# Row tiles transposed by DMA, paired last columns and an early inverse stage in a convolution and feed-forward kernel

## The chip, the cores and the metric

The kernel runs on one core of a Trainium2 chip. The metric is device time in microseconds, the median of the runs. A matrix engine (TensorE, PE in the profile), a vector engine (VectorE, DVE), an activation engine (ScalarE, ACT) and a general engine (GpSimd, POOL) work side by side, each through its own list of instructions in order; transfers are issued by one more list (SyncE, SP) and run on 16 DMA engines.

## What is computed

One layer of a sequence model over 2048 rows of 640 columns in bf16. A long convolution along the rows, done by Fourier transform, is gated by the normalised input, and a feed-forward layer of width 1728 follows:

```python
# kv = (4-tap shift of k) * v ; y = irfft(rfft(kv, 4096) * rfft(ssm_k, 4096))[:2048] + kv * ssm_D
h  = x + layernorm(x) * y
a  = einsum(layernorm(h), w1) + b1
h2 = h + einsum(a * tanh(softplus(a)), w2)
```

## The kernel before

**Tiles.** The transform is done in matmuls. A sequence of 2048 rows is split as 128 x 16; the first stage transforms over 128, the second over 16. Columns go in five chunks of 128, in three groups (two, two and one chunk). Row tile t2 is the 128 rows with the same remainder mod 16; there are 16 of them.

**The transform part.** The names are those of the operations in the code: `k1` transposes the convolution kernel on TensorE, `s1k` and `s2k` are its two transform stages, `kspe` the four shifts of k as small matmuls, `kv` the product with v on VectorE, `s1v` and `s2v` the stages of that, `prod` the product of both spectra, `i1` the inverse first stage. Each stage of matmuls writes into PSUM and is evicted as 1024 columns by ScalarE or VectorE (one helper, lines L390 and L392: the suffix `ev`). `prod` needs the kernel's spectrum twice, once with real and imaginary rows exchanged: 20 DMAs within SBUF (`d_swap`, L639) make the second copy, with real rows in partitions 0 to 63 and imaginary in 64 to 127. It runs as two instructions (L720), one for each copy. In the first stage (L510, L511) one 64-column weight is used twice, for the upper and the lower half of the output partitions. k is transposed as it is loaded, by DMA (`d_kT`, L476).

**The row chain.** For each row tile: the inverse second stage `i2pe` (L782, six matmuls into PSUM), the normalised x `lnx` on ScalarE (L789), their product `wb` on VectorE out of PSUM (L793), the sum `h` (L797), its statistics `ln2` (L802 and two more), the reciprocal root on GpSimd (L422), the normalised h `dr` (L812, into `hc`, a ring of three slots), five transposes on TensorE `trpe` (L819) and their eviction `trev` into `lnhT`.

**The feed-forward part.** Rows are taken in units of 128, 128, 256, 512, 512 and 512. For a unit, `m1pe` makes 14 chunks of 128 columns, five matmuls each (L845), ScalarE applies the activation (`hb`, L851), and `m2pe` multiplies each of the unit's row tiles by w2, 28 matmuls of 320 columns (L861); `res` adds h (L870) and a DMA stores the tile. 1728 is 13.5 x 128, so the last chunk is half zeros.

**The order.** A planner in the kernel (`_schedule`) takes operations by a table of priorities (`PRIO`) and estimated durations, picks the engine of each eviction and the PSUM bank, and emits the result; each engine's instructions then run in that order. 24 filler matmuls on zeros (`fill`, L830) may be put where TensorE is expected to be idle before the feed-forward part. All input loads, swaps and stores are on SP.

Of the kernel before, what the change touches and what calls it, by code (L numbers as in the profile page):

```python
# [17 lines left out]
D = 640  # L18
# [13 lines left out]
Q_R = "sp"  # L32
Q_V = "sp"
Q_SWAP = "sp"
KTP = 16 + S
PRIO = {
# [34 lines left out]
}  # L71
# [22 lines left out]
OFF_OB = OFF_XA + 3840  # L94

# [5 lines left out]

_CELL = {}
# [9 lines left out]
class _Op:  # L112
    __slots__ = ("name", "opts", "deps", "allocs", "emit", "prio", "lat", "start", "finish", "eng", "done", "picks", "cap", "xbar")

    def __init__(self, name, opts, deps, allocs, uses, emit, prio, lat):
        self.name = name
        self.opts = opts if isinstance(opts, list) else [opts]
        self.deps = deps
        self.allocs = list(allocs)
        for rt in list(allocs) + list(uses):  # L120
            rt.users.append(self)
        self.emit = emit
        self.prio = prio
        self.lat = lat
        self.start = None
        self.finish = None
        self.eng = None
        self.done = False
        self.cap = 0.0
        self.xbar = False  # L130

_WIN = 0.3
_SEM = 0.18
_OWN = {"act": 0.1, "dve": 0.1}
_FIRST = 0.6
_LAST_BYTE = 1.6

def _stage(name):
    m = re.match(r"(k1|s1k|s2k|kp|ks|kv|s1v|s2v|x|prod|i1|gb|d_swap|c_diag|d_kn|d_kT|d_R|d_v)(?:pe|ev)?(\d*)(?:_.*)?$", name)
    if not m:  # L140
        return name
    st = {"kp": "s2k", "x": "s2v"}.get(m.group(1), m.group(1))
    return st + m.group(2)

def _schedule(ops):
    _CELL.clear()
    free = {}
    order = []
    cap_free = 0.0
    ring_free = {}  # L150
    ring_sent = {}
    ndeps = {id(o): len(o.deps) for o in ops}
    children = {}
    for o in ops:
        for d in o.deps:
            children.setdefault(id(d), []).append(o)
    bl = {}
    for o in reversed(ops):
        m = 0.0
        for c in children.get(id(o), []):  # L160
            v = bl[id(c)] + o.lat
            if v > m:
                m = v
        bl[id(o)] = m + min(d for (_, d) in o.opts)
    ready = [o for o in ops if ndeps[id(o)] == 0]
    n_total = len(ops)
    while len(order) < n_total:
        cands = []
        for o in ready:
            t_dep = 0.0  # L170
            picks = []
            taken = set()
            for rt in o.allocs:
                best_slot = None
                for sl in rt.ring.slots:
                    if any(c in taken for c in sl):
                        continue
                    t = 0.0
                    for c in sl:
                        prev = _CELL.get(c)  # L180
                        if prev is None:
                            continue
# [744 lines left out]
```

## Time and profile before

| | us |
|---|---|
| median of 3 runs (242.58 to 244.99) | 244.71 |
| span of the profiled execution, first to last instruction | 238.7 |
| median less span | 6.0 |
| TensorE busy | 221.0 |
| VectorE busy | 155.5 |
| ScalarE busy | 139.5 |

The profile shows one execution. Busy times of TensorE include the latency of pipelined matmuls, so what one matmul costs is read from the starts of two neighbours or from the chain of waits, not from its own length. The chain follows what ended last back to its releaser, piece by piece. A group line gives count, busy time and mean length of one instruction in ns, then the idle time before it and who ended that.

### The profile page before, as it was taken

Reading aid. Unit: us, or ns where it says so; the run is one execution under the profiler, and the core shown is the slowest. Engines: PE = TensorE matmul, PEld = TensorE weight load, DVE = VectorE, ACT = ScalarE, POOL = GpSimd, SP = SyncE. Lnnn points to the kernel's source line nnn. Section 1 sums busy time; section 2 is a strip of 40 time slices with the busy share of each in tenths; the row PEclk is TensorE's granted clock in tenths of the full one; section 3 lists DMA queues with packets and bytes.
Section 4 is the critical chain, followed back from the end, with each engine's and each line's share of the span. In section 5 each row is a group of like instructions: output and inputs, shape, how many; then the busy total and the mean of one; then the engine's idle time right before and its main releaser. Section 6 shows DMA issues by size and latency. Waiting matters only on the chain.

```text
span 238.7 us, 7414 instructions
## 1 busy us (share of the span) xinstructions
PE 221.0 (93%) x3266; PEld 167.2 (70%) x3266; DVE 155.5 (65%) x318; ACT 139.5 (58%) x192; POOL 20.3 (9%) x39
## 2 busy tenths in 40 slices
PE   8888688988779999999999999999999999999993
PEld 3777577888779998698788764577744677545772
DVE  0998967899979998899999898584350332100121
ACT  2668676989998999589166456930156401366000
POOL 2500000000000003022311200210000000000000
PEclk9999999999999999999999999999999999999999
DMA  6999999806999797000000000001000001000001
GB/s 235 393 340 228 173 181 225 124 3 150 238 233 388 236 368 292 5 3 3 27 30 1 27 30 0 0 4 55 27 30 0 0 30 52 31 0 3 27 27 55
DMA packets 20049, 25.52 MB, mean 107 GB/s; under 512 B 11633, under 2 KB 15538, under 8 KB 19634
## 3 DMA queue, kind: packets, MB, share of 16 engines
q1 hardware_dynamic: 19760, 24.88, 37.5%
q8 instruction: 25, 0.41, 0.7%
q10 hardware_dynamic: 146, 0.18, 0.5%
q0 software_dynamic: 112, 0.01, 0.1%
q14 instruction: 6, 0.05, 0.1%
HBM read 14.57 MB, written 2.62 MB: 72 GB/s over the span
## 4 chain that ended last, share of the span: by engine, by line
PE 77%; ACT 10%; issue 4%; DVE 4%; DMA 3%; SPq 0%; ACTq 0%; DVEq 0%
PE banks L861 26%; PE banks L845 25%; ACT arena L390 9%; PE banks L539 6%; PE banks L731 4%; PE banks L732 4%; PE banks L782 3%; DMA arena<-tab_R 3%; PE banks L510 3%; PE banks L586 2%; DVE arena L392 2%; PE banks L819 2%; PE banks L560 1%; PE banks L830 1%; PE banks L511 1%
## 5 line engine op out<-in xcount | busy, mean ns | idle before, releaser
L390 ACT CAST arena<-banks 128x1024 bf16<-128x1024 f32 x78 | 73.2, 1046 | 16.3 <-PE banks L511 10.6
L845 PE MATMUL banks<-arena 128*128 128x512 bf16 (+2 forms) x420 | 62.3, 308 | 0.3 <-ACT arena L390 0.2
L861 PE MATMUL banks<-arena 128*128 128x320 bf16 x448 | 62.0, 299 | 0.2 <-DVE arena L793 0.2
L851 ACT ACTIVATE arena<-banks,b1s 128x512 bf16<-128x512 f32 (+2 forms) x84 | 43.5, 546 | 27.6 <-PE banks L845 25.5
L861 PEld LDWEIGHTS <-arena 128*128 128x128 bf16 x448 | 43.6, 98 | 17.1 <-issue 0.4
L845 PEld LDWEIGHTS <-arena 128*128 128x128 bf16 x420 | 35.3, 98 | 25.7 <-issue 0.7
L870 DVE TENSOR_TENSOR arena<-banks,arena 128x640 bf16<-128x640 f32 x16 | 13.2, 824 | 43.3 <-PE banks L861 43.2
L539 PE MATMUL banks<-arena 128*128 128x64 bf16 (+1 forms) x768 | 25.3, 188 | 4.6 <-ACT arena L390 2.9
L392 DVE CAST arena<-banks 128x1024 bf16<-128x1024 f32 x22 | 26.3, 1221 | 4.5 <-PE banks L511 2.2
L390 ACT COPY arena<-banks 128x640 bf16<-128x640 bf16 (+1 forms) x12 | 8.6, 746 | 32.7 <-PE banks L819 32.5
L539 PEld LDWEIGHTS <-arena 128*128 128x128 bf16 x768 | 23.3, 97 | 6.2 <-issue 5.1
L720 DVE TENSOR_TENSOR arena<-arena 128x1024 bf16<-128x1024 bf16 x40 | 24.8, 687 | 2.2 <-ACT arena L390 1.7
L510 PE MATMUL banks<-consts,arena 128*64 128x128 bf16 x320 | 21.3, 220 | 3.4 <-ACT arena L390 2.0
L511 PE MATMUL banks<-consts,arena 128*64 128x128 bf16 x320 | 21.6, 221 | 0.0
L511 PEld LDWEIGHTS <-arena 128*64 128x64 bf16 x320 | 18.4, 110 | 3.4 <-issue 3.2
L731 PE MATMUL banks<-consts,arena 128*128 128x128 bf16 x160 | 18.8, 219 | 1.3 <-DVE arena L392 0.9
L510 PEld LDWEIGHTS <-arena 128*64 128x64 bf16 x320 | 18.7, 110 | 1.7 <-issue 1.0
L732 PE MATMUL banks<-consts,arena 128*128 128x128 bf16 x160 | 18.7, 219 | 0.0
L732 PEld LDWEIGHTS <-arena 128*128 128x128 bf16 x160 | 15.6, 98 | 1.3 <-issue 1.0
L731 PEld LDWEIGHTS <-arena 128*128 128x128 bf16 x160 | 15.6, 98 | 0.6 <-issue 0.6
L789 ACT ACTIVATE arena<-arena,nmr_75,r1v 128x640 bf16<-128x640 bf16 x16 | 14.4, 926 | 2.6 <-DVE nmr_75 L684 1.4
L392 DVE COPY arena<-banks 128x1024 bf16<-128x1024 bf16 (+1 forms) x14 | 8.0, 598 | 11.8 <-PE banks L819 11.7
(47 smaller groups left out, 181.0 us busy)
## 6 DMA issues: line engine op xcount, KB each, us to landing
arena<-arena SPq DMA_DIRECT2D x20, 256.0 KB, 6.0
arena<-in_A_ssm_k_dram SPq DMA_DIRECT2D x5, 512.0 KB, 8.2
arena<-in_A_v_dram SPq DMA_DIRECT2D x2, 1280.0 KB, 15.4
arena<-in_A_q_dram SPq DMA_DIRECT2D x8, 320.0 KB, 5.6
out_dram<-arena SPq DMA_DIRECT2D x16, 160.0 KB, 1.8
arena<-in_B_w_dram SPq DMA_DIRECT2D x5, 432.0 KB, 8.4
arena<-in_B_w_dram SPq DMA_DIRECT2D x6, 320.0 KB, 4.8
arena<-tab_R SPq DMA_DIRECT2D x1, 1024.0 KB, 7.4
```

What stands on the lines that cost most here:

```text
L390: clock.append(nc.scalar.copy(o, i))
L392: nc.vector.tensor_copy(o, i)
L510: nc.tensor.matmul(ps1[0:64, gl, :], lhs, fcfs_b[:, 0, :], start=True, stop=True)
L511: nc.tensor.matmul(ps1[64:128, gl, :], lhs, fcfs_b[:, 1, :], start=True, stop=True)
L539: nc.tensor.matmul(ps2[:, c0:c0 + nd], G_t()[:, f0 + fl, :], src[:, f0 + fl, :], start=True, stop=True)
L720: nc.vector.tensor_tensor(kp, x, kp, ALU.mult)
L731: nc.tensor.matmul(pz[:, gl, :], KP_t()[:, dg, :], a12_b[:, 0, :], start=True, stop=False)
L732: nc.tensor.matmul(pz[:, gl, :], KPS_t()[:, dg, :], a12_b[:, 1, :], start=False, stop=True)
L789: nc.scalar.activation(lnx.tile, xn_t()[:, t2, :], ACT.Identity, scale=r1v[:, t2:t2 + 1], bias=nmr1[:, t2:t2 + 1])
L845: nc.tensor.matmul(ph[:, 0:w], w1_t()[:, dc, fc * P:(fc + 1) * P], lnhT_t()[:, dc, c0:c0 + w], start=(dc == 0), stop=(dc == NDC - 1))
L851: nc.scalar.activation(ub_t[u % 2]()[:, fc, 0:w], rt.tile[:, 0:w], ACT.Mish, bias=b1s[:, fc:fc + 1], scale=1.0)
L861: nc.tensor.matmul(po[:, hf2 * 512:hf2 * 512 + 320], hb[:, fc, tl * P:(tl + 1) * P], w2_t()[:, fc, hf2 * 320:(hf2 + 1) * 320], start=(fc = ...
```

## The change

Seven things change together.

- **Transposes by DMA.** For row tiles 2 to 15, `trpe` and `trev` are replaced by one DMA transpose each from `hc` into `lnhT` (`d_tr`, on SP). Tiles 0 and 1 stay on TensorE.
- **Last columns paired.** In units of more than 128 rows the last chunk is computed as 64 columns for the first half of the rows in output partitions 0 to 63 and for the second half in 64 to 127; the activation covers half the columns, and the second product takes the last 64 rows of w2 from a small tile `w2p` that holds them in either half, the rest zero. The bias of the last columns is loaded into both halves.
- **Inverse second stage ahead.** `i2pe` is split into `i2a` (groups 0 and 1, four matmuls of 256 columns for each row tile) and `i2b` (group 2, several row tiles in one bank). Their results are evicted as bf16 into SBUF (`ya`, `yb`), and `wb` reads them there. All but tile 10 stand before the first product.
- **Alternate rows.** Real and imaginary rows of the spectra alternate in the partitions; the swaps copy even to odd partitions and odd to even. The masked tables (`gb`) are written in contiguous pieces of 32.
- **`prod`** is one instruction over both copies, with the other spectrum broadcast.
- **Second product** in pieces of 512 and 128 columns; for the last row tile the two pieces are separate operations with an add and a store each.
- **Order.** Planner, priorities and fillers are gone. A written list (`ORDER`) gives each operation's engine, slot and place, and for some loads an instruction that they wait for (`pace`). Two small tiles move into the big one.

```diff
+        if t2 >= 2:
+            def trd(e, t2=t2, hc=hc):
+                return nc.sync.dma_start_transpose(lnhT_t()[:, :, t2 * P:(t2 + 1) * P], hc.tile)
+            o_td = DMA(f"d_tr{t2}", 164e3, trd, w=[("lnhT", t2)], prio=pr, after=[o_dr] + i1_pes, rate=160e3, xbar=True)
+            hc.users.append(o_td)
+            continue
...
-                    nc.tensor.matmul(ph[:, 0:w], w1_t()[:, dc, fc * P:(fc + 1) * P], lnhT_t()[:, dc, c0:c0 + w],
-                                     start=(dc == 0), stop=(dc == NDC - 1))
+                    if tail:
+                        for hh in range(2):
+                            nc.tensor.matmul(ph[64 * hh:64 * hh + 64, 0:w // 2], w1_t()[:, dc, fc * P:FF], lnhT_t()[:, dc, c0 + hh * (w // 2):c0 + (hh + 1) * (w // 2)],
+                                             start=(dc == 0), stop=(dc == NDC - 1))
+                    else:
...
-                for hf2 in range(2):
+                for a, b in parts:
                     for fc in range(NFC):
-                        nc.tensor.matmul(po[:, hf2 * 512:hf2 * 512 + 320], hb[:, fc, tl * P:(tl + 1) * P],
-                                         w2_t()[:, fc, hf2 * 320:(hf2 + 1) * 320], start=(fc == 0), stop=(fc == NFC - 1))
+                        wt = w2_t()[:, fc, a:b] if fc < NFC - 1 else w2p[:, 0, a:b]
+                        lo = tl * P
+                        if split and fc == NFC - 1 and lo >= w // 2:
+                            lo -= w // 2
+                            wt = w2p[:, 1, a:b]
+                        nc.tensor.matmul(po[:, a:b], hb[:, fc, lo:lo + P], wt, start=(fc == 0), stop=(fc == NFC - 1))
...
+        o = OP(f"i2ape{t2}", ("pe", 0.44), r=[("t2m", t2)] + [k for k in last_w if k[0] == "zb" and k[1] < 2], allocs=[rt], emit=pe, prio=41 + 0.01 * t2)
+        def yf(e, t2=t2, rt=rt):
+            return ev(e, yb(t2, 0, 512), rt.tile)
...
-            nc.vector.tensor_tensor(lnx.tile, rt.tile[:, 0:D], lnx.tile, ALU.mult)
+            return nc.vector.tensor_tensor(lnx.tile, yb(t2, 0, 640), lnx.tile, ALU.mult)
...
-                    a, b = (0, 64) if half == 0 else (64, 0)
-                    ENG_Q[Q_SWAP].dma_start(KPS_t()[a:a + 64, g0:g0 + 16, :].rearrange("p g f -> p (g f)"),
-                                      KP_t()[b:b + 64, g0:g0 + 16, :].rearrange("p g f -> p (g f)"))
+                    ENG_Q[Q_SWAP].dma_start(KPS_t()[half:P:2, g0:g0 + 16, :].rearrange("p g f -> p (g f)"),
+                                      KP_t()[1 - half:P:2, g0:g0 + 16, :].rearrange("p g f -> p (g f)"))
...
-                x = xa.tile[:, 0:nf * nd].rearrange("p (g f) -> p g f", f=nf)
-                for kt in (KP_t(), KPS_t()):
-                    kp = kt[:, d0:d1, f0:f0 + nf]
-                    nc.vector.tensor_tensor(kp, x, kp, ALU.mult)
+                x = xa.tile[:, 0:nf * nd].rearrange("p (g f) -> p g f", f=nf).unsqueeze(1).to_broadcast([P, 2, nd, nf])
+                kp = KK2_t()[:, :, d0:d1, f0:f0 + nf]
+                return (nc.gpsimd if e == "pool" else nc.vector).tensor_tensor(kp, x, kp, ALU.mult)
```

The written order around the passage into the feed-forward part and up to the fourth unit (name, engine, slots, what it waits for; some names left out):

```text
d_v1/sp// d_kT1/sp// ... d_v0/sp// d_kT0/sp// ... d_kT2/sp// ... d_kT3/sp// ... d_kT4/sp// ... d_swap0_0_48/sp//
...
i1ev1_0/act// i2bpe4/pe/0/ d_w2_12/sp//i1ev1_0 i1ev1_1/act// i2bpe0/pe/1/ ln1s2/pool// yb4/dve// i2bpe3/pe/2/ yb0/act// i2ape1/pe/3/ ln1f2/dve// yb3/dve// lnx2/act/2/ i2ape4/pe/0/ ya1/dve//
...
dr1/dve/0/ i2ape14/pe/0/ h0/dve// ya2/act// trpe1/pe/2/ ya14/act// i2ape11/pe/3/ trev1/dve// i2ape3/pe/1/ wb2/dve// ya11/act// m1pe1_6/pe/0/ ln2_0/dve//
...
dr3/dve/2/ hb0_8/act// m1pe0_4/pe/3/ ln2s_2/pool// hb0_6/act// ln1_4/dve// m1pe0_5/pe/2/ d_tr3/sp// hb0_4/act// m1pe0_3/pe/1/ hb0_5/act// m1pe1_13/pe/3/ hb0_12/act// i2ape10/pe/2/ hb0_3/act// hb1_13/act// dr2/dve/0/ m2pe0/pe/0/ ln1s4/pool// ya10/act// ln1_7/dve// d_tr2/sp//
...
dr4/dve/1/ ln2s_7/pool// ln2_6/dve// hb2_7/act// d_tr4/sp// m1pe2_10/pe/1/ hb2_4/act// m2pe1/pe/1/ dr7/dve/2/ hb2_10/act// ln2s_6/pool// ln2_5/dve// d_tr7/sp// dr6/dve/0/ ln2s_5/pool// d_tr6/sp// dr5/dve/1/ ln1_9/dve// d_tr5/sp// m2pe3/pe/0/
```

More of the change, by code (lines that the diff above doesn't have):

```diff
@@ L94 @@
 OFF_OB = OFF_XA + 3840
+NYA = 6
+OFF_YA = OFF_KK
+OFF_YB = OFF_G + 17920
 class _Ring:
@@ L247, in _schedule, with _replay @@
+        self.pace = ""
+        self.ins = None
+def _replay(ops):
+    by = {o.name: o for o in ops}
+    order = []
+    for tok in ORDER.split():
+        name, eng, slots, pace = tok.split("/")
+        o = by.pop(name)
+        o.eng = eng
+        if slots:
+            for rt, sl in zip(o.allocs, slots.split("+")):
+                rt.slot = rt.ring.slots[int(sl)]
+        o.pace = pace
+        order.append(o)
+    assert not by, sorted(by)
     return order
@@ L768, with yb, pe @@
     s1v_pes = [o for o in ops if o.name.startswith("s1vpe")]
+    s2v_pes = [o for o in ops if o.name.startswith("s2vpe")]
     prod_ops = [o for o in ops if o.name.startswith("prod")]
+    def yb(t, c0, c1):
+        off = OFF_YA + t * 1280 if t < NYA else OFF_YB + (t - NYA) * 1280
+        return view([P, D], off)[:, c0:c1]
+    for t2 in range(16):
+        rt = _RT(PB, f"i2a_{t2}")
+        def pe(e, t2=t2, rt=rt):
+            py = ps_alloc(rt)
+            for grp in range(2):
+                d0, d1 = GRP_DG[grp]
+                for ri in range(2):
+                    nc.tensor.matmul(py[:, 4 * d0:4 * d1], t2m_t()[:, t2, ri, :], zb_t[grp]()[:, ri, t2, :], start=(ri == 0), stop=(ri == 1),
+                                     skip_group_check=True)
+        o = OP(f"i2ape{t2}", ("pe", 0.44), r=[("t2m", t2)] + [k for k in last_w if k[0] == "zb" and k[1] < 2], allocs=[rt], emit=pe, prio=41 + 0.01 * t2)
+        def yf(e, t2=t2, rt=rt):
+            return ev(e, yb(t2, 0, 512), rt.tile)
+        OP(f"ya{t2}", EV(512), w=[("ya", t2)], uses=[rt], emit=yf, prio=41 + 0.01 * t2, after=[o] + (s1v_pes if t2 < NYA else s2v_pes))
@@ new lines, with pe, yf @@
+    TB = [(0, 2), (2, 4), (4, 8), (8, 12), (12, 16)]
+    for bi, (a, b) in enumerate(TB):
+        rt = _RT(PB, f"i2b_{bi}")
+        def pe(e, a=a, b=b, rt=rt):
+            py = ps_alloc(rt)
+            d0, d1 = GRP_DG[2]
+            for t2 in range(a, b):
+                for ri in range(2):
+                    nc.tensor.matmul(py[:, (t2 - a) * 128:(t2 - a + 1) * 128], t2m_t()[:, t2, ri, :], zb_t[2]()[:, ri, t2, :], start=(ri == 0), stop=(ri == 1),
+                                     skip_group_check=True)
+        o = OP(f"i2bpe{bi}", ("pe", 0.113 * (b - a)), r=[("t2m", t) for t in range(a, b)] + [k for k in last_w if k[0] == "zb" and k[1] == 2], allocs=[rt], emit=pe, prio=62 + bi)
+        def yf(e, a=a, b=b, rt=rt):
+            if a < NYA < b:
+                ev(e, view([P, NYA - a, D], OFF_YA + a * 1280)[:, :, 512:640], rt.tile[:, 0:(NYA - a) * 128].rearrange("p (t d) -> p t d", d=128))
+                return ev(e, view([P, b - NYA, D], OFF_YB)[:, :, 512:640], rt.tile[:, (NYA - a) * 128:(b - a) * 128].rearrange("p (t d) -> p t d", d=128))
+            off = OFF_YA + a * 1280 if b <= NYA else OFF_YB + (a - NYA) * 1280
+            return ev(e, view([P, b - a, D], off)[:, :, 512:640], rt.tile[:, 0:(b - a) * 128].rearrange("p (t d) -> p t d", d=128))
+        OP(f"yb{bi}", EV(128 * (b - a)), w=[("yb", t) for t in range(a, b)], uses=[rt], emit=yf, prio=62 + bi, after=[o])
@@ L822, in trev @@
         def trev(e, t2=t2, rtt=rtt):
-            ev(e, lnhT_t()[:, :, t2 * P:(t2 + 1) * P], rtt.tile[:, 0:640].rearrange("p (c t) -> p c t", c=NDC))
+            return ev(e, lnhT_t()[:, :, t2 * P:(t2 + 1) * P], rtt.tile[:, 0:640].rearrange("p (c t) -> p c t", c=NDC))
         OP(f"trev{t2}", EV2(640), w=[("lnhT", t2)], uses=[rtt], emit=trev, prio=pr, after=[o_tr] + i1_pes)
-    for i in range(24):
-        rt = _RT(PB, f"fill{i}")
-        def fill(e, rt=rt):
-            nc.tensor.matmul(ps_alloc(rt), warm[:, 0:128], warm[:], start=True, stop=True)
-        OP(f"fill{i}", ("pe", 0.22), allocs=[rt], emit=fill, prio=900, after=i1_pes)
     ub_t = [lambda: big("ub0", [P, NFC, 512], OFF_UB0), lambda: big("ub1", [P, NFC, 512], OFF_UB1)]
@@ L847 @@
-            o = OP(f"m1pe{u}_{fc}", ("pe", 5 * (0.003 + w / 2400.0)), r=[("w1", c) for c in range(NDC)] + [("lnhT", t) for t in t2s], allocs=[rt], emit=pe, prio=100 + u,
+                    if tail:
[3 more added lines that the diff above has]
+                    else:
+                        nc.tensor.matmul(ph[:, 0:w], w1_t()[:, dc, fc * P:(fc + 1) * P], lnhT_t()[:, dc, c0:c0 + w],
+                                         start=(dc == 0), stop=(dc == NDC - 1))
@@ L848, with hbf @@
+            we = w // 2 if tail else w
+            o = OP(f"m1pe{u}_{fc}", ("pe", 5 * (0.003 + we / 2400.0)), r=[("w1", c) for c in range(NDC)] + [("lnhT", t) for t in t2s], allocs=[rt], emit=pe, prio=100 + u,
                    after=m2.get(u - 2, ()))
-            def hbf(e, u=u, fc=fc, rt=rt, w=w):
-                nc.scalar.activation(ub_t[u % 2]()[:, fc, 0:w], rt.tile[:, 0:w], ACT.Mish, bias=b1s[:, fc:fc + 1], scale=1.0)
-            OP(f"hb{u}_{fc}", ("act", _act_d(w) + 0.05), r=["b1s"], w=[("ub", u % 2, fc)], uses=[rt], emit=hbf, prio=60 + u, after=[o] + i1_pes)
+            def hbf(e, u=u, fc=fc, rt=rt, we=we, tail=tail):
+                bi = NFC if tail else fc
+                return nc.scalar.activation(ub_t[u % 2]()[:, fc, 0:we], rt.tile[:, 0:we], ACT.Mish, bias=b1s[:, bi:bi + 1], scale=1.0)
@@ L873 @@
-            od = DMA(f"d_out{t2}", 164e3, (lambda e, t2=t2, ob=ob: nc.sync.dma_start(oview[:, t2, :], ob.tile)), prio=100 + u, after=[o3], rate=340e3)
-            ob.users.append(od)
-        c0 += w
-    for o in ops:
-        o.prio = PRIO.get(o.name, PRIO.get(_stage(o.name), o.prio))
-    order = _schedule(ops)
-    seq = {id(o): i for i, o in enumerate(order)}
-    order.sort(key=lambda o: (o.start, seq[id(o)]))
-    t_mlp = min(o.start for o in order if o.name == "m1pe0_0")
-    order = [o for o in order if not (o.name.startswith("fill") and o.start > t_mlp)]
+                        wt = w2_t()[:, fc, a:b] if fc < NFC - 1 else w2p[:, 0, a:b]
@@ new lines, in pe2, with resf @@
+                        lo = tl * P
[3 more added lines that the diff above has]
+                        nc.tensor.matmul(po[:, a:b], hb[:, fc, lo:lo + P], wt, start=(fc == 0), stop=(fc == NFC - 1))
+            ob = _RT(R_OB, f"ob{t2}")
+            o2 = None
+            for a, b in ([(0, 512), (512, 640)] if last else [(0, 640)]):
+                nm = f"{t2}" + ("ab"[a > 0] if last else "")
+                o2 = OP(f"m2pe{nm}", ("pe", 3.82 * (b - a) / 640), r=[("w2", c) for c in range(NFC)] + [("ub", u % 2, fc) for fc in range(NFC)], allocs=[rt] if a == 0 else [], uses=[rt] if a else [],
+                        emit=(lambda e, f=pe2, a=a, b=b: f(e, parts=((a, b),))) if last else pe2, prio=100 + u + 0.5, after=[o2] if o2 else [])
+                def resf(e, t2=t2, rt=rt, ob=ob, a=a, b=b):
+                    if a == 0:
+                        slot(R_OB, ob, "ob", [P, D], OFF_OB, 1280)
+                    return nc.vector.tensor_tensor(ob.tile[:, a:b], rt.tile[:, a:b], xn_t()[:, t2, a:b], ALU.add)
+                o3 = OP(f"res{nm}", ("dve", 0.16 + (b - a) * 0.00104), r=[("x", t2)], allocs=[ob] if a == 0 else [], uses=[rt] + ([ob] if a else []), emit=resf, prio=100 + u + 0.5, after=[o2] + prod_ops)
+                od = DMA(f"d_out{nm}", 164e3 * (b - a) / 640, (lambda e, t2=t2, ob=ob, a=a, b=b: nc.sync.dma_start(oview[:, t2, a:b], ob.tile[:, a:b])), prio=100 + u, after=[o3], rate=340e3)
+                ob.users.append(od)
@@ L884 @@
+            m2.setdefault(u, []).append(o2)
+        c0 += w
     info = mybir.DependencyInfo(mybir.DependencyClass.Sync, mybir.DependencyReason.DATA)
[L885 removed]
+    by = {o.name: o for o in ops}
     with tc.manual_schedule():
[L887 removed]
+        for o in _replay(ops):
             if o.emit is None:
                 continue
[L890 to L897 removed]
```

331 lines of the change are left out of this document (133 added, 198 removed), and 34 rows, old and new, of the table PRIO.

## The prediction

> **What bounds the kernel now.** I read the page first, then the windows by stage, the chain of waits in order of time, and last the groups by shape. The page's busy line names TensorE; two windows say where this holds. The first is the transform part (sum and mean of twelve windows from 0 to 95.5 us), the second the feed-forward part (window, TensorE busy, count, clock, DMA).
>
> ```profile
> span 238.7 us, 7414 instructions
> PE 221.0 (93%) x3266; PEld 167.2 (70%) x3266; DVE 155.5 (65%) x318; ACT 139.5 (58%) x192; POOL 20.3 (9%) x39
> ...
> sum 95.50, PE 82.14 PEld 74.35 DVE 80.32 ACT 77.28 POOL 7.37; mean PE 6.85 PEld 6.20 DVE 6.69 ACT 6.44 POOL 0.61
> ...
> 101.50:234.90 133.40, 132.94 (x1015) 1.00 0.05 20
> ```
>
> Up to 95.5 us TensorE, VectorE and ScalarE are each busy for 77 to 82 us; none is the bound, and what is lost is idle time in turns. From 101.5 to 234.9 us TensorE is busy for 132.9 of 133.4 us at full clock, so there each instruction taken off it is worth its full length. The chain shows what it does besides the two matrix products, and the passage between the two parts:
>
> ```profile
> 94.51 1.08 PE banks L830 x5
> 95.60 1.10 PE banks L782 x12
> ...
> 97.13 0.71 PE banks L782 x6
> 97.84 1.94 PE banks L830 x9
> 99.78 0.69 PE banks L782 x6
> 100.47 0.29 PE banks L819 x5
> ...
> 101.53 1.50 PE banks L845 x24
> ...
> 120.53 7.64 PE banks L845 x70
> 128.17 0.28 PE banks L819 x5
> 128.45 0.55 PE banks L782 x6
> 129.00 3.80 PE banks L861 x28
> ...
> 204.55 15.11 PE banks L845 x70
> 219.66 15.23 PE banks L861 x112
> ...
> 234.91 0.82 DVE arena L870
> ```
>
> L782 is the inverse second stage, 6 matmuls and 0.55 us for one row tile; L819 the transpose, 5 and 0.28 us; L830 the fillers; L845 the first and L861 the second product. Four row tiles of L782 and one of L819 are done before 101.53 us.
>
> The span is 238.7 us and the median of the runs 244.71, so 6.0 us lie around it (3.9 by the fastest run, 6.3 by the slowest). I add 6.0.
>
> **Feed-forward part: the gain.** (1) Twelve of the 16 inverse tiles leave it: 12 x 0.55 = 6.6 us. One, tile 10, stays with its four wide matmuls: without the two narrow ones at 0.056 each (rows below) 0.44 us. Net 6.2. (2) Fifteen of the 16 TensorE transposes stood in it, 15 x 0.28 = 4.2 us; tile 0 alone stays, so 3.9. (3) The last 64 columns: a unit of 512 rows takes 15.11 / 14 = 1.08 us for each chunk of 128 columns, the unit of 256 rows 7.64 / 14 = 0.55. The tail chunk becomes two matmuls of half the rows in the two halves of the output partitions. Whether two such run together is in the trace already, at the first transform stage, whose pairs are built so (lines L510 and L511):
>
> ```profile
> 59.86 0.22 PE L510 MATMUL banks<-consts,arena 128*64 128x128 bf16 x1
> 59.86 0.22 PE L511 MATMUL banks<-consts,arena 128*64 128x128 bf16 x1
> 59.92 0.22 PE L510 MATMUL banks<-consts,arena 128*64 128x128 bf16 x1
> 59.92 0.22 PE L511 MATMUL banks<-consts,arena 128*64 128x128 bf16 x1
> ...
> 94.40 0.06 PE banks L731
> 94.46 0.05 PE banks L732
> ```
>
> Both halves start together, one pair each 0.055 us, as long as one full matmul of the same width takes (L731, L732: 0.056). So the tail halves: 3 x 0.54 + 0.27 = 1.9 us; if they ran in turn, nothing. Sum of (1) to (3): 12.0 us. (4) The second product goes from 28 matmuls of 320 columns (3.80 us) to 14 of 512 and 14 of 128: 14 x 15.11 / 70 + 14 x 0.056 = 3.02 + 0.78 = 3.80; nothing.
>
> **The passage: given back.** Between 94.51 and 101.53 us stand 2.5 us of inverse tiles, 0.3 of transpose, 3.5 of fillers and 0.7 of waiting, 7.0 in all. Now 15 tiles and the narrow part of tile 10 stand there, 16 x 0.55 - 0.44 = 8.4, and one transpose, 0.3. They hide only if their results leave PSUM as fast:
>
> ```profile
> 73.17 18.43 ACT L390 CAST arena<-banks 128x1024 bf16<-128x1024 f32 x20 [0.84 <-DVE arena L392]
> ...
> L597 DVE TENSOR_TENSOR arena<-banks,arena 128x512 bf16<-128x512 f32 x20 | 12.4, 683 | 1.6 <-PE banks L586 1.0 <-issue 0.6
> L797 DVE TENSOR_TENSOR arena<-arena 128x640 bf16<-128x640 bf16 x16 | 7.8, 489 | 0.4
> L812 DVE TENSOR_SCALAR arena<-arena,mv_76,r_77 128x640 bf16<-128x640 bf16 x16 | 7.1, 441 | 3.3 <-POOL r_77 L422 3.3
> L789 ACT ACTIVATE arena<-arena,nmr_75,r1v 128x640 bf16<-128x640 bf16 x16 | 14.4, 926 | 2.6 <-DVE nmr_75 L684 1.4
> ...
> 101.79 0.89 DVE L802 BATCH_NORM_STATS2 st_72<-arena 128x6 f32<-128x320 bf16 x2
> ...
> 103.03 0.88 DVE L676 BATCH_NORM_STATS2 st_72<-arena 128x6 f32<-128x320 bf16 x2
> ```
>
> ScalarE: 18.43 / 20 = 0.92 us per 1024 columns, so ten evictions of 512 (0.46 each), three of the narrow kind (1.2 together) and two normalisations (0.9 each) make 7.6 us. VectorE by the new order, up to the first transposed tile: six evictions at 0.64, two multiplies and two adds at 0.49 (the multiply now reads SBUF only, like L797), a statistics group (from 101.79 to 103.03, 1.2), one L812 at 0.44, a copy at 0.45, 7.9 us. Both lie just under TensorE's 8.7; adding 0.5 of waiting gives 9.2 against 7.0, 2.2 us given back. Bounds: 1.7 with no wait, 5 if each of the two engines makes TensorE wait by turns for a third of its work.
>
> **The transform part: little.** By the order written out, ScalarE has 76 of its 100 evictions of 1024 columns instead of 78, VectorE 24 instead of 22 (2.4 us more) and one copy of the first transpose fewer (0.6 less). The 20 pairs of products become single instructions of twice the length. The price:
>
> ```profile
> L720 DVE TENSOR_TENSOR arena<-arena 128x1024 bf16<-128x1024 bf16 x40 | 24.8, 687 | 2.2 <-ACT arena L390 1.7 <-DMA arena<-arena 0.5
> ...
> 27.72 2.48 DVE L597 TENSOR_TENSOR arena<-banks,arena 128x512 bf16<-128x512 f32 x4 [0.58 <-issue]
> ...
> 4.60 0.82 SPq L486 DMA_DIRECT2D arena<-in_A_v_dram  x2
> 5.46 25.24 SPq L476 DMA_TRANSPOSE arena<-in_A_k_dram  x4
> 31.75 8.61 SPq L639 DMA_DIRECT2D arena<-arena  x8
> ...
> 8.00:16.00 8.00, 5.99 (x146) 5.49 (x140) 7.79 (x17) 6.13 (x7) 3.22 (x4) 1.00 1.03 376
> ```
>
> From 640 to 1024 columns L797 and L720 differ by 198 ns, 0.52 ns a column, so 2048 take 1.22 us against 2 x 0.62 of pitch; with about 0.08 saved at each boundary 1.6 us for 20. VectorE's load is then as before, and the gain can only come from idle time. Its first product with v starts at 27.72 us; k's first transpose stands behind both loads of v on SP. The new order puts it between them: 1.31 MB less ahead of it, 3.5 us at 376 GB/s, while the rest of v lands some 3 us later, behind that transpose. I take 2.0 us. Bounds: 6 gained (four tenths of VectorE's 95.5 - 80.3 = 15.2 us of idle time), 5 lost, if the fixed order lets that grow by a third. The swaps of partition halves by alternate rows cost nothing here: the only wait for them is the 0.5 us in L720's row; a slower rate would show there.
>
> **The end and the rest.** The last add shrinks from 640 to 128 columns: 825 ns less 512 x (825 - 683) / 128, some 250 ns; 0.6 us gained, the add of the first 512 lying beside the last 14 matmuls, and its output DMA too. The cleared 2 x 640 columns and two more tiny bias DMAs go to POOL, busy for 20.3 of 238.7 us; behind them waits the shift table, first needed by the matmuls ahead of L597 at 27.72 us. Nothing, unless POOL were held that long.
>
> **The DMA transposes: late or not.** Fourteen new DMAs on SP, each behind its L812 instruction. No row shows one from SBUF; the nearest is that of k, 16 blocks of 128 x 128 each:
>
> ```profile
> L476 SPq DMA_TRANSPOSE arena<-in_A_k_dram x5: 2628/3498/16050, 5.5 to 40.4; - x5
> ...
> DMA to landing us min/median/max: 5.1/6.4/7.1
> ...
> out_dram<-arena SPq DMA_DIRECT2D x16, 160.0 KB, 1.8
> ```
>
> Issue scales with blocks: 5/16 of 2.63 = 0.8 us, and 5.1 - 2.6 = 2.5 us after it, 3.3 to landing. Bounds: 1.8 (the output of the same bytes) and 6.4 (the whole of k's). I take 3.3, as the work is a third of k's. With the start of the first product as zero, VectorE reaches the end of the second L812 of tiles 2 and 3 at 9.9 us (five statistics groups of 1.2, two multiplies and two adds at 0.49, an eviction at 0.64, three of L812 at 0.44), so the tile lands at 13.2; TensorE needs it after 28 chunks at 0.29, a transpose, tile 10 and one second product, 8.2 + 0.3 + 0.4 + 3.8 = 12.7. That is 0.5 us lost. Tiles 4 to 7: 13.9 us more on VectorE and 3.3, 27.1, against 13.2 + 7.4 + 7.6 = 28.2, hidden by 1.1. Tiles 8 to 11 have 6 us to spare. hc has three slots, so the last L812 of tiles 4 to 7 waits for the first one's transpose, 3.3 us earlier in the order: just met. Behind it wait the next statistics and two output adds.
>
> The sum: -12.0 + 2.2 - 2.0 - 0.6 + 0.5 = -11.9, a span of 226.8 and a time of 232.8 us. Its own range, without the rivals, is 228 to 237.5.
>
> **Rivals.** A. The transposes land late but overlap, 6.4 us each: tile 2 at 16.3, 3.1 us more; the slot wait of hc puts 3.1 on the last of tiles 4 to 7, 26.9 + 6.4 = 33.3 against 31.3, 2.0 more: 237.9 us. For it: k's landing times; against: they are for 3.2 times the bytes.
>
> B. The slower side: the transposes go one at a time, at s us each, with SP held. Six of them from 8.3 us on feed tiles 2 to 7, so the two first delays make 2s - 4.4 and 4s - 15, together 6s - 19.4. The gain without the waiting is 12.4, so it decides from s = 5.3. At k's 6.4, with 3.4 each at the next two units, 25.8 us: 258 us. Against it: k's four issues in a row took 25.2 us with the first held 16.05 behind v, so three in 9.2, some 3 us each of k's size.
>
> The Trainium skill speaks for B: its page "VectorE: DVE Perf Modes", section "The three transpose paths", gives 1309 ns for a 128 x 128 block by DMA against 390 on TensorE; by it five blocks in a row are 6.5 us (an estimate), much as at 6.4. The trace disagrees so far: 16 blocks of k landed in 5.1 to 7.1 us, not 21.
>
> C. The order written out loses ahead of the feed-forward part: the transform part 5 us longer instead of 2 shorter, 239.8 us. For it: three engines at 81 to 86% there, so any late producer is seen; against: the loads of k come sooner.
>
> D. The change does not do what it says at the tail, its halves running in turn: 1.9 us more, 234.7. Against: the pairs at 59.86.
>
> **How the numbers follow.** Forecast 0.61, A 0.13, C 0.12, D 0.05, B 0.09. About 1% (2.4 us) is what a measurement of this kernel can tell from no change. The forecast, A, D and most of C lie under 242.3 us: faster 0.84. C with the passage's upper bound, 239.8 + 2.8 = 242.6, lies within 1%: 0.05. B, and the rest of C, 0.11, is slower. The range goes from 226.2 (6 gained in the transform part, the passage at its best, 3.9 around the span) to 243 (C with the passage).
>
> **What would show it.** Right: between the first and the last matmul of the two products some 122 us, not 133.4; no inverse matmuls in it but four; tail pairs starting together, 0.107 us apart in large units; the transposes some 3.3 us to landing; a passage of 9 us; VectorE's last add 0.25 us. Wrong: idle TensorE before the products of tiles 2 and 3 or 4 to 7 that ends with a DMA into lnhT (A, B), or a last eviction of the inverse first stage later than 95.5 us (C).

## The result and the profile after

The changed kernel takes 299.81 us (median of 4 runs, 298.79 to 300.51), the kernel before 244.11 (median of 4 runs): a ratio of 1.231, 95% interval 1.222 to 1.239. The forecast of 232.8 us has the wrong sign. The page of the changed kernel, with span, busy times, TensorE's slices and its granted clock:

```profile
span 297.0 us, 7285 instructions
PE 223.4 (75%) x3184; PEld 162.3 (55%) x3197; DVE 153.4 (52%) x302; ACT 139.4 (47%) x197; POOL 23.1 (8%) x41
...
PE   8685834572004925774829999999999999999995
...
PEclk9999985796557795999568999999999999999999
```

TensorE, VectorE, ScalarE and GpSimd are busy as long as before within 3 us; what is longer is idle time, in the first 22 slices of 7.4 us, ahead of about 163 us. From there on TensorE is busy without a break. The same stretch in both kernels, first before, then after (window, length, busy time and count of TensorE, weight loads, VectorE, ScalarE, GpSimd, then clock, DMA share, GB/s):

```profile
20.00:95.00 75.00, 64.86 (x1883) 60.68 (x1878) 66.49 (x105) 65.40 (x71) 2.36 (x8) 1.00 0.88 215
```

```profile
20.00:95.00 75.00, 33.72 (x992) 31.04 (x987) 29.05 (x35) 26.84 (x29) 0.00 (x0) 0.75 0.40 107
```

TensorE does 52% of what it did in that stretch, VectorE 44 and ScalarE 41%, and the transfers' share falls from 0.88 to 0.40. No engine and no transfer is the bound there; everything waits. The waits of the changed kernel say for what (engine, line, releaser; us in total, times, longest). L322 is the eviction, L521 the shifts of k (`kspe`), L532 the product with v (`kv`), L653 `prod`:

```profile
ACT arena L322 <- DMA arena<-arena: 49.4, 11, 7.2
...
PE banks L521 <- DMA arena<-arena: 23.8, 2, 15.6
DVE arena L653 <- DMA arena<-arena: 21.7, 4, 9.1
...
DVE arena L532 <- DMA arena<-arena: 14.4, 3, 6.2
DVE arena L322 <- DMA arena<-arena: 13.3, 2, 7.6
DVE arena L653 <- DMA arena<-in_B_w_dram: 12.1, 3, 4.4
```

A transfer from `arena` to `arena` is in this stretch a swap. Before, all waiting for swaps was 0.5 us. Now `kv`, which reads the shifted k from PSUM and v, waits for swaps of the kernel's spectrum, and `prod` waits for loads of w2, which it never reads. VectorE's timeline of the changed kernel (start, length, line, ..., in brackets the idle time ahead and its releaser):

```profile
44.11 1.29 DVE L532 TENSOR_TENSOR arena<-banks,arena 128x512 bf16<-128x512 f32 x2 [6.15 <-DMA arena<-arena]
48.89 1.29 DVE L532 TENSOR_TENSOR arena<-banks,arena 128x512 bf16<-128x512 f32 x2 [3.49 <-DMA arena<-arena]
54.90 2.48 DVE L532 TENSOR_TENSOR arena<-banks,arena 128x512 bf16<-128x512 f32 x4 [4.72 <-DMA arena<-arena]
...
79.27 1.22 DVE L653 TENSOR_TENSOR arena<-arena 128x2048 bf16<-128x2048 bf16 x1 [6.05 <-DMA arena<-arena]
89.64 1.22 DVE L653 TENSOR_TENSOR arena<-arena 128x2048 bf16<-128x2048 bf16 x1 [9.14 <-DMA arena<-arena]
```

The instruction lists of the two programs, which exist before anything runs, say the same. Waits are written per range of a tile, and the whole work area is one tile, `arena`. Before, one instruction of `kv` waits for a transfer (its v), three of `prod` (once a group) and two of ScalarE's evictions. After the change it is four, seven and eleven, and two of VectorE's evictions. The lists also name what is waited for: the three new waits of `kv` are for swaps of the first group; the products of the first group wait for swaps of the second and third, those of the second and third for loads of w2. The swaps wait in their turn for evictions and products, and are issued from 39.5 to 112.4 us, where before it was 31.8 to 65.5.

Two parts of the change alter the ranges: the swaps' rows are taken with a step of two partitions, and `prod` names both copies of the spectrum in one view, from KP to KPS. Both are theories of waits that no data asks for. W1 is the stepped rows, W2 the merged view; the first expectations, written when W1 alone was in sight, say W. The rivals are O, the written order itself is slower; K, k's transpose between the loads of v; and P, stepped partitions make the transfer itself slow.

### The profile page after: what moved, and what is told of

It reads as the page before. It is cut to its first block, busy times and chain, and to the rows that moved or that the text cites. A ratio compares the mean times of both kernels' runs of the same rounds, so it can differ in the third digit from the quotient of the medians.

```text
span 297.0 us, 7285 instructions
## 1 busy us (share of the span) xinstructions
PE 223.4 (75%) x3184; PEld 162.3 (55%) x3197; DVE 153.4 (52%) x302; ACT 139.4 (47%) x197; POOL 23.1 (8%) x41
## 4 chain that ended last, share of the span: by engine, by line
PE 52%; DMA 17%; DVE 14%; SPq 6%; issue 5%; ACT 4%; POOL 0%; DVEq 0%; ACTq 0%
PE banks L843 19%; PE banks L819 16%; DMA arena<-arena 11%; DVE arena L653 6%; SPq L410 5%; PE banks L665 4%; PE banks L664 3%; DVE arena L322 3%; ACT arena L322 3%; DMA arena<-in_A_v_dram 3%; PE banks L521 2%; DMA arena<-in_B_w_dram 2%; PE banks L473 2%; PE banks L719 2%; PE banks L444 2%
## 5 line engine op out<-in xcount | busy, mean ns | idle before, releaser
L322 ACT CAST arena<-banks 128x1024 bf16<-128x1024 f32 (+2 forms) x91 | 80.4, 938 | 78.8 <-DMA arena<-arena 49.4
L843 PE MATMUL banks<-arena 128*128 128x512 bf16 (+1 forms) x408 | 60.2, 297 | 0.4
L843 PEld LDWEIGHTS <-arena 128*128 128x128 bf16 x448 | 35.0, 98 | 27.7
L653 DVE TENSOR_TENSOR arena<-arena 128x2048 bf16<-128x2048 bf16 x20 | 24.0, 1222 | 38.3 <-DMA arena<-arena 21.7
L322 DVE CAST arena<-banks 128x1024 bf16<-128x1024 f32 (+1 forms) x31 | 33.2, 1098 | 19.4 <-DMA arena<-arena 13.3
L473 PE MATMUL banks<-arena 128*128 128x64 bf16 (+1 forms) x768 | 29.9, 199 | 16.6 <-ACT arena L322 7.7
L854 DVE TENSOR_TENSOR arena<-banks,arena 128x640 bf16<-128x640 f32 (+2 forms) x17 | 13.3, 785 | 51.0 <-PE banks L843 50.8
L444 PE MATMUL banks<-consts,arena 128*64 128x128 bf16 x320 | 23.5, 228 | 11.9 <-ACT arena L322 7.8
L664 PE MATMUL banks<-consts,arena 128*128 128x128 bf16 x160 | 24.0, 246 | 10.3 <-DVE arena L653 10.3
L521 PE MATMUL banks<-diagm,arena 32*128 32x128 bf16 (+3 forms) x380 | 8.5, 251 | 25.6 <-DMA arena<-arena 23.8
L665 PE MATMUL banks<-consts,arena 128*128 128x128 bf16 x160 | 23.3, 246 | 3.8 <-DVE arena L653 3.8
L664 PEld LDWEIGHTS <-arena 128*128 128x128 bf16 x160 | 18.1, 113 | 10.5 <-DVE arena L653 10.5
L521 PEld LDWEIGHTS <-arena 32*128 32x128 bf16 x380 | 8.0, 152 | 26.1 <-issue 25.8
L532 DVE TENSOR_TENSOR arena<-banks,arena 128x512 bf16<-128x512 f32 x20 | 12.6, 683 | 16.7 <-DMA arena<-arena 14.4
L665 PEld LDWEIGHTS <-arena 128*128 128x128 bf16 x160 | 17.9, 113 | 4.7 <-DVE arena L653 4.7
```

The source lines that it names most:

```text
L322: copied[0] = nc.scalar.copy(o, i) if eng == "act" else nc.vector.tensor_copy(o, i)
L444: nc.tensor.matmul(ps1[0:64, gl, :], lhs, fcfs_b[:, 0, :], start=True, stop=True)
L473: nc.tensor.matmul(ps2[:, c0:c0 + nd], G_t()[:, f0 + fl, :], src[:, f0 + fl, :], start=True, stop=True)
L521: nc.tensor.matmul(outs[i // 2][:, i % 2, src + j0:src + j1, :], lhs, diagm[rows, dc * 4 + j0:dc * 4 + j1, :], start=(src == -3), stop=(sr ...
L653: return (nc.gpsimd if e == "pool" else nc.vector).tensor_tensor(kp, x, kp, ALU.mult)
L664: nc.tensor.matmul(pz[:, gl, :], KP_t()[:, dg, :], a12_b[:, 0, :], start=True, stop=False)
```

## The experiments

Five of the kernels below (e2, e3, e4, e8, e9) were executed once each. What is read from them are distances of 17 to 51 us; the kernel before ranged from 239.8 to 247.9 us beside them.

**Rows in halves again** (e1): the tables and the swaps as before, everything else as changed.

```diff
-  dma_start(KPS_t()[half:P:2, g0:g0 + 16, :], KP_t()[1 - half:P:2, g0:g0 + 16, :])
+  a, b = (0, 64) if half == 0 else (64, 0)
+  dma_start(KPS_t()[a:a + 64, g0:g0 + 16, :], KP_t()[b:b + 64, g0:g0 + 16, :])
```

> The changed kernel with real and imaginary rows put back into the lower and upper 64 partitions; the swaps copy whole halves again. All else of the change stays. Theory W (false waits): a copy whose partitions are taken with a step of two is treated as touching other columns of the big tile too, so each swap waits for unrelated evictions and later work on unrelated columns waits for the swap; the swaps' stretch, 39.5 to 112.9 us in the changed kernel, goes back to about 35 us long and the time falls from 299.8 to 228 to 237 us (the forecast's own range). Theory O (order): the written order itself starves the transform part; then the time stays over 280 us. Theory K: k's DMA transpose put between the loads of v costs a drain of the queue; then 5 to 10 us of it stays and the time is 238 to 245 us.

Measured 273.98 us (272.89 to 275.34), a ratio to before of 1.133 [1.120, 1.146]: 26 us come back, not all, and the time lies in none of the three ranges. The waits of `kv` and `kspe` for swaps are gone from the trace. Those of `prod` (L656 here) are not:

```profile
DVE arena L656 <- DMA arena<-arena: 19.2, 5, 5.6
PEld L475 <- issue: 17.2, 9, 9.7
PEld L667 <- DVE arena L656: 15.2, 3, 9.1
PE banks L667 <- DVE arena L656: 14.8, 3, 8.9
...
DVE arena L656 <- DMA arena<-in_B_w_dram: 13.5, 3, 6.3
```

So one false wait was found and a second stands behind it: the inverse first stage (L667) waits for `prod`, and `prod` for swaps and for weights.

**Alternate rows alone** (e2): the kernel before with the stepped tables and swaps and nothing else.

```diff
-  dma_start(KPS_t()[a:a + 64, g0:g0 + 16, :], KP_t()[b:b + 64, g0:g0 + 16, :])
+  dma_start(KPS_t()[half:P:2, g0:g0 + 16, :], KP_t()[1 - half:P:2, g0:g0 + 16, :])
```

> The kernel before with the alternate rows alone (tables, masked tables, swaps), its order unchanged. Theory W: the swaps wait and are waited for as in the changed kernel, 285 to 310 us. Theory O: within 3 us of the kernel before, about 244 us.

294.19 us, 51 more than the kernel before beside it (243.39). The written order isn't in this kernel, so O has no part in it. Its waits show the same new releasers (L388 the eviction, L595 `kv`):

```profile
ACT arena L388 <- DMA arena<-arena: 54.2, 12, 8.7
...
DVE arena L595 <- DMA arena<-arena: 24.6, 5, 6.4
```

**Halves, but stepped copies** (e3): e1 with each swap cut into two copies of every second row of a half, so the data lie in halves and only the views step.

```diff
+  for s in range(2):
+      dma_start(KPS_t()[a + s:a + 64:2, g0:g0 + 16, :], KP_t()[b + s:b + 64:2, g0:g0 + 16, :])
```

> As e1, the data in halves, but each swap is issued as two copies of 32 partitions taken with a step of two (even and odd ones of the half). Theory W: the step alone brings the waits back, 285 to 320 us. Theory P (ports: alternate rows load the memory's ports otherwise): about 5 us over e1, for 20 more small copies, so under 245 us.

311.48 us, 37.5 more than e1. The tables and the masked tables are those of before here, so it isn't the order of the rows that costs but the stepped view of them. (There are 40 copies here instead of 20, so 37.5 us isn't the price of the step alone; e2 has 20.) P would have to show in the landing times of the swaps. Of e1 (first) and e3 (second), with count, KB each, us from issue to landing:

```profile
arena<-arena SPq DMA_DIRECT2D x20, 256.0 KB, 3.8
```

```profile
arena<-arena SPq DMA_DIRECT2D x40, 128.0 KB, 2.3
```

The stepped copies land quickly, and so do the stepped swaps of 256 KB in the changed kernel (2.4 us, against 6.0 before, when more transfers were under way). Nothing of P shows in them.

**The work area in two tiles** (e4): the changed kernel with `arena` cut in two behind the spectra and k's transposed copy; no instruction, order or size changes.

```diff
-  arena = pool.tile([P, OFF_END // 2], BF16, name="arena")
+  low = pool.tile([P, OFF_G // 2], BF16, name="low")
+  high = pool.tile([P, (OFF_END - OFF_G) // 2], BF16, name="high")
```

> The changed kernel with alternate rows, the big tile cut into two at the end of k's transposed copy, so that v, the spectra's first stage, the products with v and the weights w1 lie in another tile than the swapped copies; the transposed k and the spectra stay in the swaps' tile. Theory W: only the evictions of the second stage and the shifts of k wait falsely, 250 to 285 us, between e1 and the changed kernel. Theory P: 295 to 300 us, as the changed kernel.

282.16 us, 17.6 less. `kv` writes into `high`, the swaps work in `low`: its waits for swaps are gone, ScalarE's fall from 49.4 to 22.3 us, and what shares `low` with the swaps (evictions, the shifted reads of k, `prod`) still waits:

```profile
ACT low L324 <- DMA low<-low: 22.3, 4, 7.3
PEld L523 <- issue: 21.0, 4, 11.2
PE banks L523 <- DMA low<-low: 19.3, 2, 11.1
DVE low L655 <- DMA low<-low: 18.3, 5, 6.5
```

If the waits had been for data, or the transfers themselves slow, a cut between tiles could not have taken them away. P falls.

**Two products, alternate rows** (e8) is the changed kernel with the edit below; **the merged product alone in the kernel before** (e9) is its reverse:

```diff
-  kp = KK2_t()[:, :, d0:d1, f0:f0 + nf]
-  return nc.vector.tensor_tensor(kp, x_twice, kp, ALU.mult)
+  for kt in (KP_t(), KPS_t()):
+      kp = kt[:, d0:d1, f0:f0 + nf]
+      r = nc.vector.tensor_tensor(kp, x, kp, ALU.mult)
```

> The changed kernel with the product as two instructions, alternate rows kept. If the stepped rows alone make waits (W1), 285 to 297 us: at kv and at kspe waits of several us for swaps remain. If the merged product were behind most of the loss, 230 to 260.

> The kernel before with the product merged to one instruction and nothing else. If its one range over both copies makes it wait for later groups' swaps and loads (W2), 262 to 280 us. If it costs only its own length, 242 to 245.

(`x_twice` stands for the other spectrum broadcast over both copies.) 282.82 us for e8, a little under what W1 expected. The waits of `kspe` (L521) and `kv` (L532) are as long as in the changed kernel; those of `prod` for weights are gone, those for swaps are not (21.6 us):

```profile
PE banks L521 <- DMA arena<-arena: 23.9, 2, 15.7
...
DVE arena L532 <- DMA arena<-arena: 14.3, 3, 6.2
```

273.5 us for e9, 30 more than before, from one edit of three lines. Its `prod` (busy, mean ns, then idle time ahead and its releasers):

```profile
L719 DVE TENSOR_TENSOR arena<-arena 128x2048 bf16<-128x2048 bf16 x20 | 24.0, 1223 | 33.3 <-DMA arena<-arena 17.5 <-DMA arena<-in_B_w_dram 9.8 <-PE banks L731 4.5
```

The instruction itself is as quick as forecast, 1.22 us; 33.3 us of idle time stand ahead of it, against 2.2 ahead of the 40 single ones before. By its instruction list eight of the 20 wait for transfers (before, three of 40): the first of them for the swaps of its own group, four more of the first group for swaps of the second and third, one of the second group for a swap of the third, and two for loads of w2.

**Rows in halves, two products** (e7): both undone, the other five parts of the change in.

> The changed kernel with rows back in halves and the product as two instructions again: all else of the change is in (DMA transposes, paired tail, inverse second stage ahead, the written order). If false waits of the stepped rows and of the merged product are the whole of the loss (W1 and W2), the transform part is back to about the time of before and the forecast of the other parts stands: 228 to 237.5 us, last eviction of the inverse first stage at 94 to 98 us, and the groups' waits for transfers at the product under 1 us each. If the written order itself loses (O), 240 to 262: then the products or kv still wait several us at a time.

237.40 us (234.44 to 238.31), ratio 0.976 [0.967, 0.986]: faster than the kernel before, by 1.4 to 3.3%. The instruction list again has one, three and one waits for transfers at `kv`, `prod` and ScalarE's evictions, and `prod` waits for no transfer in the trace:

```profile
L657 DVE TENSOR_TENSOR arena<-arena 128x1024 bf16<-128x1024 bf16 x40 | 24.9, 688 | 1.0 <-ACT arena L324 0.7
```

The time is at the upper edge of what was expected, and the last matmul of the inverse first stage ends at 100.9 us, where 94 to 98 was expected for its last eviction. Together the two false waits account for 62 of the 67 us between forecast and measured time. With this the two causes stand in a square (us; 282.8, 294.2 and 273.5 are single executions):

| | rows in halves | alternate rows |
|---|---|---|
| the changed kernel, two products | 237.4 | 282.8 |
| the changed kernel, one product | 274.0 | 299.8 |
| the kernel before, two products | 243.4 to 244.1 | 294.2 |
| the kernel before, one product | 273.5 | not run |

The stepped rows alone cost 45 us in the changed kernel, the merged product alone 37, both together 62: some of the waiting is the same time.

**Tail not paired** (e10), on e7:

```diff
-  split = w > P
+  split = False
```

> As e7_halves_two, but the last 64 feed-forward columns aren't paired: one chunk of full width on 64 output partitions. If pairs run together, as the prediction has it, 1.9 us more than e7_halves_two (1.5 to 2.3), and the first product of a large unit takes 0.54 us longer. If they run in turn, no difference.

237.93 us, ratio 0.979 [0.970, 0.988], which the times cannot tell from e7. The traces can, as TensorE is busy throughout: from the first matmul of the two products to the end of the chain's last piece of them e10 takes 111.9 to 235.18, 123.3 us, e7 110.0 to 232.27, 122.3, both at a granted clock of 1.00. Pairing is worth 1.0 us, between the two expectations. The chain of e7 shows where the rest goes, at the tail of a large unit (first two rows) and in 49 full matmuls of another (third):

```profile
151.35 0.67 PE banks L821 x10
152.02 1.19 PE banks L824 x5
...
190.44 10.74 PE banks L824 x49
```

10.74 / 49 is 0.219 a matmul. Five pairs take 0.67, not 5 x 0.107 = 0.54, and the five full ones behind them 1.19 instead of 1.10: 0.34 us gained in each of three large units.

**Both loads of v first** (e11): e7 with the second load of v ahead of k's first transpose again.

```diff
-  d_v1/sp// d_kT1/sp// ... d_v0/sp//
+  d_v1/sp// d_v0/sp// d_kT1/sp//
```

> e7_halves_two with one change: both loads of v stand ahead of k's first transpose on SP, as they do in the kernel before. In e7_halves_two the last matmul of the inverse first stage ends 6.3 us later than in the kernel before (100.9 against 94.5 us), the second load of v is issued at 18.0 us instead of 5.0 and the transposes of k end at 36.7 us. If this place of the load is what loses (K), the inverse first stage ends at 94 to 97 us and the time is 230.5 to 234.5 us, what the prediction's other terms give. If the rest of the written order loses (O), the inverse first stage still ends at 99 to 102 us and the time stays at 235.5 to 239 us.

235.57 us (234.52 to 238.02), ratio 0.978 [0.971, 0.984]; by the times no different from e7. In the two profiled executions the inverse first stage ends 3 us earlier, at 97.8 instead of 100.9 us. The matmul groups of it, of e7 and of e11 (min/median/max ns, first and last start):

```profile
L669 PE MATMUL banks<-consts,arena x160: 217/219/231, 75.5 to 100.7; 128*128 128x128 bf16 x160
```

```profile
L669 PE MATMUL banks<-consts,arena x160: 216/219/230, 73.5 to 97.8; 128*128 128x128 bf16 x160
```

At 97.8 us the stage lies between the two theories' ranges, and the time is at the low end of O's. The 3 us may be K's, about half of the 6.4 by which e7's transform part is longer than before, but that is not shown: e10 runs the same instructions as e7 up to there and starts its last matmul of the stage at 102.8 us, 2 later than e7, so single executions differ by nearly as much.

**The first group's chunk 0 ahead of the second group's chunk 2** (e12), on e11, and **its first transform stage ahead too** (e13), on e12:

```diff
-  kspe2/pe/3+0+1/ ... kv2_0/dve// ... kv2_1/dve// ... kspe0/pe/3+2+2/ ... kv0_0/dve// ... kv0_1/dve//
+  kspe0/pe/3+0+1/ ... kv0_0/dve// ... kv0_1/dve// ... kspe2/pe/3+2+2/ ... kv2_0/dve// ... kv2_1/dve//
```

> e11_v_first with two operations exchanged in the written order: the four shifts of k and the product with v of chunk 0 (first group) take the places of those of chunk 2 (second group), which stood ahead of them. In e11_v_first the last matmul of the inverse first stage ends at 97.8 us, 3.3 us later than in the kernel before, and the second kv of the first group starts at 42.05 us against 32.63. If the written order's putting the second group ahead of the first is what is left of the loss (O1), the inverse first stage ends 1 to 3 us earlier, 95 to 97 us, and the time falls by as much, to 232.5 to 235. If it is spread over the order (O2), nothing changes by more than 0.7 us: 235 to 236.5.

> e12_kv0_first, and the first transform stage of chunk 0's product with v (four groups of matmuls and their evictions) ahead of four second stages of the kernel's spectrum of the second group. By O1 the first product of the spectra, at 53.85 us in e11_v_first against 45.34 before, starts 3 us earlier or more, and the inverse first stage ends at 94 to 96 us, 231 to 234.5 us. By O2 the second group then waits in its place and the time stays at 235 to 237.

236.45 us, 0.974 [0.969, 0.980], and 236.70 us, 0.978 [0.971, 0.984]. The inverse first stage ends at 99.1 and 99.7 us, not earlier, so nothing of O1 shows. What is left of the loss, some 3 us, is spread over the written order, lies in something not tried or is the difference between two executions; it stays open.

## Why the prediction was wrong

By the parts of the forecast, from the traces' own marks (last matmul of the inverse first stage, first and last matmul of the two products, end):

| stage | before | after | after - before | forecast | e7 - before |
|---|---|---|---|---|---|
| transform part, to the last matmul of the inverse first stage | 94.5 | 162.9 | +68.4 | -2.0 | +6.4 |
| passage, to the first product | 7.0 | 8.8 | +1.8 | +2.2 | +2.1 |
| the two products | 133.4 | 122.3 | -11.1 | -12.0 | -11.1 |
| from there to the end | 3.8 | 3.0 | -0.8 | -0.6 | -0.8 |
| transposes late | | 0 | 0 | +0.5 | 0 |
| span | 238.7 | 297.0 | +58.3 | -11.9 | -3.4 |

*The step that failed is the transform part, twice.* The prediction said that the swaps by alternate rows "cost nothing here", since their only wait was 0.5 us and a slower rate would show there. It looked at how long the transfer takes and not at who is made to wait for it: e2 shows 50 us for that sentence. And it priced the merged `prod` by its length, 1.22 us, which is exact (1222 ns), and took 1.6 us as saved. The view that makes one instruction of two also makes one range of what had been two, with the columns of other groups in between: e9 shows 30 us for it. The bounds of the term, 6 gained to 5 lost, came from idle time that was already there, so no false wait could be in them. Both could be seen without a run, in the waits of the changed program's own instructions.

Rival C had the place right, ahead of the products, and a sign that the prediction gave for it came true (the inverse first stage later than 95.5 us). Its price, 5 us, was for a lost order, and its mechanism isn't what happened. What C meant would be seen in e7, where the false waits are out: +6.4 us between the two profiled executions. These lie 3.4 us apart, while the ratio of 0.976 makes 5.8 us of some 242. So about 2 us of the 6.4, an estimate from these figures, come from which executions were profiled.

*k's transpose between the loads of v.* SP let go of the transpose earlier, at 17.9 us in e7 against 21.5, the 3.5 us forecast. But it landed only 18.1 us after its issue, at 23.8 us, and the shifts that read it start at 23.9 us, where before they started at 24.5: 0.6 us gained. And "the rest of v lands some 3 us later" was 6. SP's queue of e7, the landing of k's transposes, of which the first is the longest, and VectorE's first product with v:

```profile
5.33 0.33 SPq L422 DMA_DIRECT2D arena<-in_A_v_dram  x1
5.70 12.23 SPq L412 DMA_TRANSPOSE arena<-in_A_k_dram  x1
17.99 0.58 SPq L422 DMA_DIRECT2D arena<-in_A_v_dram  x1
...
DMA to landing us min/median/max: 5.5/6.2/18.1
...
28.19 2.49 DVE L534 TENSOR_TENSOR arena<-banks,arena 128x512 bf16<-128x512 f32 x4 [3.26 <-DMA arena<-in_A_v_dram]
```

The second load stood behind the 12.23 us that SP spent on the transpose, and its landing ended VectorE's wait at 28.2 us; before, it had landed by 21.8 (5.0 + 16.8). So the first product with v starts 0.5 us later than the 27.7 of before, where the term had counted on an earlier start. The queue's holding time had been quoted, as 16.05 us of the first transpose, and was not put into this term.

*The products.* Right to 0.9 us. The miss is the tail (D was half right: the halves run together, but a pair takes 0.134 us, not 0.107, and delays what follows). 122.3 without the pair's 1.0 is 123.3: the inverse tiles and transposes are worth 10.1, as forecast. Of the changed kernel the first product's matmuls, the last piece of the second product in the chain and the last adds:

```profile
L819 PE MATMUL banks<-arena x395: 216/273/390, 171.7 to 263.1; 128*128 128x512 bf16 x95, 128*128 128x128 bf16 x70, 128*128 128x256 bf16 x33
...
286.62 7.35 PE banks L843 x54
...
293.21 1.07 DVE L854 TENSOR_TENSOR arena<-banks,arena 128x512 bf16<-128x512 f32 x2 [2.20 <-PE banks L843]
```

*The transposes.* A and B fall. All fourteen land alike, so the estimate of 3.3 us to landing was on the safe side, and the product waits for none. SP is held for 1.2 us by each, not the 0.8 that came of taking the issue in proportion to the blocks:

```profile
L784 SPq DMA_TRANSPOSE arena<-arena x14: 1199/1207/1264, 179.5 to 236.6; - x14
...
DMA to landing us min/median/max: 2.6/2.6/2.6
```

The Trainium skill's "VectorE: DVE Perf Modes", section "The three transpose paths", with its 1309 ns for a block of 128 x 128, would give five blocks 6.5 us (an estimate); the 2.6 us measured for five disagree, and the measurement decides.

*Around the span.* The prediction added 6.0 us, the distance of one profiled execution from the median of other runs. Where time and span are of the same execution, 1.8 us lie around it (298.79 and 297.0 here, 237.13 and 235.3 in e7, 240.50 and 238.7 in a run of the kernel before). The other 4.2 was the spread between runs. e7's span is 8.5 us over the forecast's 226.8, 8.4 of it the transform part; its time, 237.1 in that execution, is only 4.3 over 232.8, by luck: the forecast had those 4.2 too many.

## What to carry to other kernels

Before pricing a change of a view (a step over partitions, a dimension merged over two buffers in one tile), list which instructions newly wait for which, for the program's waits follow the range that a view spans, not the elements that it touches; two tiles, or two instructions, can be cheaper than one. When an order is written by hand, look at how long each transfer holds the queue (12.2 us here): a load behind it is issued that much later. And read a loss against both kernels: of the seven parts here two cost 62 us together, and the other five make the kernel 2.4% faster [1.4, 3.3].

## What the runs showed that was not expected

The granted clock of the changed kernel fell in the idle stretch, to a mean of 0.75 from 20 to 95 us with TensorE busy for 33.7 us; before, it was 1.00 there with 64.9. The total busy time hardly changed (223.4 against 221.0 us), and what grew is idle time, so the lower clock isn't what made the kernel slower. A DMA transpose of five blocks from SBUF holds SP for 1.2 us and lands after 2.6, while the first one of sixteen blocks from HBM held it for 12.2 behind the load of v (the shortest of the five for 2.3).
